# Seven transposed tiles by DMA instead of TensorE, one score step moved, and PSUM banks of pair 2 dealt anew, in a fused attention and phase-mixing kernel

## The chip, the cores and the metric

The kernel runs on one core of a Trainium2 chip. The metric is the device time of one execution in microseconds (us); of several runs the median is taken. The core's engines are TensorE (PE, matrix products), VectorE (DVE), ScalarE (ACT) and GpSimd (POOL); SyncE (SP) issues DMAs. Each engine works through its own list of instructions in order, and semaphores hold an instruction back until what it needs is done.

## The reference

Eight batches, 576 tokens, 8 heads of 64, so a model width of 512. First comes attention within chunks of 64 tokens, then a token mixer with phases and a channel product:

```python
scores = (1/8) * q_c @ k_c^T            # within each chunk of 64 tokens, per head
attn = softmax(scores)
x = (attn @ v_c), heads side by side     # (8, 576, 512)

theta = x @ w_theta
zr, zi = x * cos(theta), x * sin(theta)
y = w_tok_r @ zr + w_tok_i @ zi          # over the 576 tokens
u = x + y
out = u + max(u @ w_ch, 0)
```

## The kernel before, in words

The eight batches are taken as four pairs, 0 to 3. The two batches of a pair hold 2 x 576 tokens, that is nine tiles of 128 tokens: tiles 0 to 3 are the first batch, 4 to 7 the second, and tile 8 holds the last 64 tokens of both. The attention half works in groups of such tiles, A, B, C, D (two tiles each) and M (tile 8). The second half works by tile. Operands are fp16 and sums fp32.

The order of the work is written out by hand. `ORDER`, at the top of the file, is a list of steps such as `V1.2D.3`: a kind of step, the pair, the group or the tile, and a PSUM bank or a buffer slot. The steps are issued as they stand there, each engine receives its share in that order, and nothing reorders them. Moving a step in the list therefore moves it on its engine and on no other. The kinds that matter here, with the lines on which the profile shows them:

- `qk`, `v`: loads of a group, issued by POOL with a cast to fp16 (L170, L165, L210).
- `T`: DVE transposes queries and keys of a group (L332). `S`: TensorE makes the scores, in small tiles of 32 x 64 of its array, 64 products for a full group (L351). `E`: ACT takes the exponentials (L380).
- `V0`, `V1`: TensorE multiplies with the values, four heads each (L397, also in smaller array tiles). `N0`, `N1`: DVE takes the reciprocals (L412) and divides (L414); that gives x.
- `X`: TensorE transposes x into PSUM (L434), and `xa` or `xv` copies it out (L459, L457); or `xd`, one DMA transpose from SBUF to SBUF, issued by SP (L451).
- `H`: theta on TensorE (L472). `G`: cosine and sine on ACT (L491). `Z`: DVE multiplies x by both (L507 to L514).
- `Y`: the token product of a tile, nine TensorE products of 128x512 (L537). `A`: DVE adds x, which makes u in the place of x (L549).
- `U`: TensorE transposes u in four blocks into PSUM (L554), and `ua` (ACT, L566) or `uv` (DVE, L564) copies it out; or `ud`, one DMA transpose issued by SP (L562).
- `W`: the channel product, four TensorE products (L577). `R`: DVE takes the maximum with 0 and adds u (L589). `st`, `sg`, `sa`: the store, issued by SP, POOL or ACT (L605, L602).

The `U` and `ud` ways to the transposed u are these:

```python
    def u_t(p, j, b):
        ps = banks(b, 1, FP16)[:, 0:DM].rearrange("p (a c) -> p a c", c=P)
        for a in range(NDB):
            nc.tensor.transpose(ps[:, a, :], st["x", p][:, j, a * P : a * P + P], id16)
...
            if engine == "d":
                nc.sync.dma_start(uT, st["x", p][:, j], transpose=True)
```

PSUM has eight banks, all dealt by the numbers in `ORDER`. A step that writes a bank waits until the step that read the bank last is done. `S`, `H` and `X` of a full group use one or two banks, from the number given on. Because the two halves of the kernel overlap, the second half of pair 1 (`Y`, `U`, `W`, `R` of tiles 10 to 18, the first digit being the pair) runs between the attention steps of pairs 2 and 3. In the list before, the tiles of pair 1 are all transposed on TensorE; those of pairs 2 and 3 (but 38) by DMA. SP's list is short: stores of pair 0 and 1, the x transposes of 2C and 2D, then the u transposes of pair 2 and so on. ACT needs another function table for `E` than for `G`, and loads it whenever the kind changes (L140).

Of the kernel before, what the change touches and what calls it, by code (L numbers as in the profile page):

```python
# [48 lines left out]
A.26 E.3B.2 v.3D sa.11 ud.23.2 ud.21.4 W.16.4 A.25 R.16.1 W.13.2 V1.3D.0 R.13.2 V1.3A.6 V0.3A.3
N1.3D ua.12.1 N0.3A st.16 sa.13 xd.3M.0 N1.3A Y.24.5 A.24 Y.27.2 A.27 W.12.0 R.12.4 V0.3D.3  # L50
V1.3B.6 V0.3B.1 N1.3B xd.3A.3 ud.20.3 N0.3B N0.3D Y.28.5 V1.3C.6 V0.3C.0 A.28 W.14.2 H.3M.3
G.3M.0 R.14.0 xd.3B.1 ud.25.5 N0.3C H.3A.4 xd.3D.2 G.3A.1 W.21.2 N1.3C R.21.3 W.23.0 Z.3A H.3B.6
G.3B.2 sg.17 Z.3M ud.24.6 W.25.1 sa.21 R.23.5 xd.3C.0 H.3D.2 ud.28.7 W.20.4 H.3C.5 ud.22.1
G.3D.1 R.25.1 Z.3B Y.30.0 G.3C.0 Z.3D ud.26.0 sg.12 Z.3C Y.31.7 R.20.2 A.30 A.31 Y.36.1 Y.35.2
W.22.3 A.35 R.22.4 Y.33.5 W.28.6 A.33 Y.34.4 sg.23 A.34 ud.35.4 R.28.3 ud.31.2 W.26.0 Y.32.7
Y.37.2 W.35.3 A.36 ud.33.5 R.26.5 W.31.5 A.32 A.37 Y.38.4 ud.34.3 ud.30.1 st.26 ud.36.7 sa.20
sg.25 sa.28 R.35.1 R.31.2 ud.32.0 A.38 ud.27.4 sg.14 W.34.6 W.36.1 U.38.2 W.30.0 W.33.7 sg.31
sa.35 ua.38.3 R.34.0 ud.37.2 R.30.3 st.30 W.27.2 sa.34 R.36.5 sg.22 R.33.6 sg.36 R.27.2 W.32.3
R.32.4 W.38.5 R.38.0 sg.32 st.33 st.27 sx.38 W.24.4 R.24.3 sa.24 W0.37.6 R0.37.1 W1.37.0 R1.37.2
sa1.37 st0.37  # L60
""".split()


# [611 lines left out]
```

## Time and profile before

| | |
|---|---|
| Median of 3 runs | 191.35 us (191.06 to 191.56) |
| The profiled execution's own time | 190.84 us |
| Its span, first to last instruction | 189.0 us |
| Granted TensorE clock over the span | 0.997 |
| TensorE busy | 181.8 us, 96% |
| DVE / ACT / POOL busy | 136.8 / 95.3 / 89.7 us |
| Transposes of u on TensorE (L554) | 76 |
| DMA transposes of u / of x, issued by SP | 17 / 7 |

Lines named Lnn are lines of the kernel before. "PE" in the profile is the matrix product, "PEld" the load of its stationary operand, which overlaps. A product's length as printed holds the time of the pipeline too: products follow each other more closely than they are long, so costs are taken from one start to the next. A bracket in a row gives the idle time before it and the instruction that ended it.

### The profile page before, as it was taken

What the parts mean: (1) busy time and instruction counts of PE and PEld (TensorE: products, weight loads), DVE (VectorE), ACT (ScalarE), POOL (GpSimd) and SP (SyncE); (2) the same over time, 40 slices, a digit from 0 to 9 for tenths busy, and PEclk for the clock granted to TensorE, in tenths of its full rate; (3) what the DMA queues carried; (4) which work ended last, traced back from release to release, by engine and by line L of the source; (5) the groups of instructions that cost most, each with busy time, mean ns of one, the idle gap of its engine ahead of it and who ended that gap; (6) DMA issues with size and microseconds to landing.
All of it is one profiled execution on the core that took longest, in us unless ns stands there. A gap on an engine that the chain in (4) does not pass through costs nothing.

```text
span 189.0 us, 6110 instructions
## 1 busy us (share of the span) xinstructions
PE 181.8 (96%) x2649; PEld 93.8 (50%) x2649; DVE 136.8 (72%) x259; ACT 95.3 (50%) x124; POOL 89.7 (47%) x129
## 2 busy tenths in 40 slices
PE   7999999999999999999999999999999999999990
PEld 2446555654566465545554555465454444444440
DVE  0527886889798999699877867963987965455480
ACT  3247995276566993586109984695304680000100
POOL 8874986698876898997386410100010020000220
PEclk9999999999999999999999999999999999999998
DMA  5999999999999999999999990921457861238975
GB/s 151 295 189 173 180 172 170 190 177 169 199 187 181 192 148 224 178 144 174 212 147 175 179 129 10 243 80 63 141 140 141 183 206 59 41 78 186 266 272 186
DMA packets 98682, 31.34 MB, mean 166 GB/s; under 512 B 90336, under 2 KB 94304, under 8 KB 98656
## 3 DMA queue, kind: packets, MB, share of 16 engines
q0 software_dynamic: 75952, 18.11, 98.2%
q1 hardware_dynamic: 20560, 9.18, 20.3%
q10 hardware_dynamic: 2144, 3.67, 6.0%
q8 instruction: 20, 0.33, 0.7%
q14 instruction: 6, 0.05, 0.1%
HBM read 33.06 MB, written 9.44 MB: 225 GB/s over the span
## 4 chain that ended last, share of the span: by engine, by line
PE 74%; DMA 9%; DVE 6%; POOL 5%; issue 3%; ACT 1%; POOLq 0%; DVEq 0%
PE psum L537 31%; PE psum L577 13%; PE psum L472 13%; DMA land<-in_k_dram 8%; PE psum L154 7%; PE psum L351 4%; POOL v L210 3%; PE psum L397 3%; DMA v<-in_v_dram 2%; PE psum L554 2%; DVE T L332 1%; PE psum L284 1%; PE psum L434 1%; DVE o L589 1%; DVE x L549 1%
## 5 line engine op out<-in xcount | busy, mean ns | idle before, releaser
L537 PEld LDWEIGHTS <-wT 128*128 128x128 f16 (+1 forms) x360 | 30.7, 100 | 34.0 <-issue 1.5
L210 POOL DMA_DIRECT2D v<-in_v_dram x56 | 41.7, 763 | 11.2 <-DMA land<-in_k_dram 7.9
L537 PE MATMUL psum<-zr,wT 128*128 128x512 f16 (+1 forms) x180 | 45.4, 381 | 0.4 <-DVE x L549 0.3
L537 PE MATMUL psum<-zi,wT 128*128 128x512 f16 (+1 forms) x180 | 43.1, 379 | 0.0
L605 POOL DMA_DIRECT2D out_dram<-o x10 | 5.5, 554 | 69.4 <-DVE o L589 49.7
L549 DVE TENSOR_TENSOR x<-psum,x 128x512 f16<-128x512 f32 x36 | 24.5, 683 | 17.0 <-PE psum L537 16.3
L577 PE MATMUL psum<-wch,uT 128*128 128x512 f16 (+1 forms) x148 | 35.2, 374 | 0.0
L472 PE MATMUL psum<-wtheta,xT 128*128 128x512 f16 x144 | 34.1, 380 | 0.2 <-ACT xT L459 0.2
L589 DVE SCALAR_TENSOR_TENSOR o<-psum,x 128x512 f32<-128x512 f32 (+1 forms) x37 | 24.4, 671 | 9.5 <-PE psum L577 5.4
L491 ACT ACTIVATE cos<-psum,pihalf 128x1024 f16<-128x1024 f32 (+1 forms) x22 | 21.2, 963 | 16.3 <-PE psum L472 16.2
L332 DVE STREAM_TRANSPOSE T<-land 64x256 f32<-64x256 f32 (+3 forms) x38 | 26.9, 723 | 1.8 <-DMA land<-in_k_dram 1.4
L380 ACT ACTIVATE eT<-psum 128x1024 f16<-128x1024 f32 (+1 forms) x22 | 18.4, 864 | 19.0 <-PE psum L351 19.0
L414 DVE TENSOR_TENSOR x<-psum,recip 128x512 f16<-128x512 f32 (+1 forms) x40 | 25.5, 638 | 1.4
L566 ACT COPY uT<-psum 128x512 f16<-128x512 f16 x15 | 8.5, 593 | 32.5 <-PE psum L554 31.5
L472 PEld LDWEIGHTS <-xT 128*128 128x128 f16 x144 | 13.4, 98 | 15.6 <-ACT xT L459 0.3
L577 PEld LDWEIGHTS <-uT 128*128 128x128 f16 x148 | 13.7, 98 | 14.6 <-issue 0.4
L140 ACT ACT_TABLE_LOAD x14 | 18.0, 1283 | 4.1 <-DVE recip L412 3.1
L491 ACT ACTIVATE sin<-psum 128x1024 f16<-128x1024 f32 (+1 forms) x22 | 19.1, 870 | 0.0
L170 POOL DMA_DIRECT2D land<-in_q_dram x15 | 13.6, 907 | 5.6 <-DVE o L589 2.3
L154 PE MATMUL psum<-zeros 128*128 128x512 f16 x51 | 14.5, 445 | 1.2 <-DVE pihalf L145 1.2
L170 POOL DMA_DIRECT2D land<-in_k_dram x15 | 13.6, 904 | 1.7 <-DMA land<-in_k_dram 1.3
L351 PEld LDWEIGHTS <-T 32*64 32x64 f16 x1152 | 10.6, 105 | 4.7 <-DVE T L332 1.9
(40 smaller groups left out, 141.9 us busy)
## 6 DMA issues: line engine op xcount, KB each, us to landing
land<-in_q_dram POOLq DMA_DIRECT2D x15, 256.0 KB, 6.8
land<-in_k_dram POOLq DMA_DIRECT2D x15, 256.0 KB, 7.3
out_dram<-o SPq DMA_DIRECT2D x11, 256.0 KB, 2.7
v<-in_v_dram POOLq DMA_DIRECT2D x40, 64.0 KB, 6.2
out_dram<-o ACTq DMA_DIRECT2D x10, 256.0 KB, 2.9
out_dram<-o POOLq DMA_DIRECT2D x10, 256.0 KB, 3.2
v<-in_v_dram POOLq DMA_DIRECT2D x16, 128.0 KB, 6.9
land<-in_moe_w_theta_dram SPq DMA_DIRECT2D x2, 512.0 KB, 7.4
```

What stands on the lines that cost most here:

```text
L154: nc.tensor.matmul(banks(b), zeros[:, 0:P], zeros)
L170: nc.gpsimd.dma_start(t[:, w].rearrange("p h s d -> p h (s d)"), ap[2 * p + bb, :, s0 : s0 + GT, :].rearrange("h (p s) d -> p h (s d)", s=2),)
L210: nc.gpsimd.dma_start(v16[rows, slot + t, :, 0:D], v[b, :, t0 : t0 + m, :].rearrange("h s d -> s h d"),)
L332: nc.vector.transpose(to.bitcast(FP32).rearrange("p (x l s) -> p x s l", l=32, s=2), src.bitcast(FP32).rearrange("p (x s d) -> p x s d", s ...
L380: nc.scalar.activation(out=to, in_=ps, func=AF.Exp, scale=scale)
L414: nc.vector.tensor_tensor(out=x.rearrange("p r (h d) -> p r h d", h=H // 2), in0=ps[:, :, :, 0:D], in1=recip[:, 0:n].broadcast_to((P, n, H ...
L472: nc.tensor.matmul(ps[:, (j - js[0]) * DM : (j - js[0] + 1) * DM], xT[:, j, a, :], wtheta16[:, a, :], start=(a == 0), stop=(a == NDB - 1),)
L491: nc.scalar.activation(out=t[:, js[0] : js[-1] + 1].rearrange("p j e -> p (j e)"), in_=ps, func=AF.Sin, bias=bias, scale=1.0,)
L537: nc.tensor.matmul(ps[half[c]] if j == MID else ps, wT[:, kt, t0 : min(t0 + P, S)], z, start=(b is not None and i == 0), stop=(i == len(kt ...
L549: nc.vector.tensor_tensor(out=x, in0=st.pop(("ps_y", p, j)), in1=x, op=ALU.add)
L577: nc.tensor.matmul(ps, uT[:, a, :], wch16[:, a, cols[f]], start=(a == 0), stop=(a == NDB - 1),)
L589: nc.vector.scalar_tensor_tensor(out=o, in0=ps, scalar=0.0, in1=st["x", p][:, j, cols[f]], op0=ALU.max, op1=ALU.add,)
```

## The change

Only `ORDER` is changed; the functions are the same, and the file is one line shorter, so that L562 becomes L561 and so on.

1. For the tiles 10, 11, 12, 13, 14, 16 and 17 of pair 1, the step `U` and its copy `ua` or `uv` are taken out, and `ud` is put in with the same slot. Five of them (10, 11, 16, 13, 14) stand in a row after `xd.2C`, which itself moves up ahead of `H.2B`; `ud.17` follows `A.17`, and `ud.12` follows `W.17`. `st.05`, a store that stood ahead of `xd.2C`, is now behind `ud.17` on SP. Tiles 15 and 18 stay on TensorE.
2. `S.3B` and `E.3B` move up from behind `S.3A` and `Y.26` to behind `Y.21`, ahead of `Z.2C`, `Y.22` and the scores 3D and 3A. `R.15` moves up to ahead of `Y.20`.
3. Around pair 2's values and x: `Y.15` writes bank 7 (was 2), `X.2A` writes bank 4 (was 2); `A.14` moves behind `A.15`; each of `N0.2B`, `N1.2B` and `N0.2A` now follows its `V` in the list; `U.18` and its copy move behind `X.2A`; `V1.3M` moves from behind `Y.18` to behind `U.18`.

The part of the list that changes, cut to it:

```diff
-V0.2M.4 N0.2M v.2C V1.2C.2 V1.2M.5 W.07.0 qk.3A.11 N1.2C N1.2M R.07.2 qk.2D.12 Y.18.6 V1.3M.7
-V0.2C.0 A.18 N0.2C S.2B.4 E.2B.1 Y.14.2 A.14 V0.2B.3 V1.2B.5 V0.2A.0 N0.2B Y.15.2 U.18.3 N1.2B
-N0.2A A.15 uv.18.2 qk.3C.0 v.2D X.2B.5 X.2M.6 xa.2B.2 xa.2M.3 X.2A.2 v.3B xa.2A.0 H.2B.0 T.3C.0
-T.2D.2 G.2B.1 qk.3B.1 W.18.3 R.18.3 H.2A.5 U.15.4 Y.17.2 U.10.3 H.2M.0 Z.2B G.2A.2 ua.15.4
-ua.10.3 N1.3M G.2M.0 S.3C.5 Z.2A A.17 S.2D.3 E.2D.2 W.15.1 U.17.7 Z.2M Y.20.2 uv.17.1 V1.2D.3
-E.3C.1 A.20 V0.3M.0 V0.2D.5 st.05 Y.23.7 xd.2C.1 N1.2D A.23 N0.2D T.3B.1 U.14.2 U.11.3 sa.18
-N0.3M xd.2D.2 W.17.4 ua.11.5 U.16.7 R.15.4 st.07 Y.21.3 A.21 R.17.5 qk.3D.3 v.3C v.3A H.2C.5
-ua.16.6 T.3A.0 W.10.7 ua.14.0 G.2C.1 T.3D.2 H.2D.0 G.2D.2 Y.22.2 Z.2C R.10.0 S.3D.3 S.3A.5 st.15
-E.3A.3 S.3B.0 E.3D.0 Z.2D Y.26.7 sg.03 U.12.5 A.22 U.13.2 sa.10 ua.13.7 W.11.6 R.11.3 Y.25.3
-A.26 E.3B.2 v.3D sa.11 ud.23.2 ud.21.4 W.16.4 A.25 R.16.1 W.13.2 V1.3D.0 R.13.2 V1.3A.6 V0.3A.3
-N1.3D ua.12.1 N0.3A st.16 sa.13 xd.3M.0 N1.3A Y.24.5 A.24 Y.27.2 A.27 W.12.0 R.12.4 V0.3D.3
+V0.2M.4 N0.2M v.2C V1.2C.2 V1.2M.5 W.07.0 qk.3A.11 N1.2C N1.2M R.07.2 qk.2D.12 Y.18.6 V0.2C.0
+A.18 N0.2C S.2B.4 E.2B.1 Y.14.2 V0.2B.3 N0.2B V1.2B.5 N1.2B V0.2A.0 N0.2A Y.15.7 A.15 A.14
+qk.3C.0 v.2D X.2B.5 X.2M.6 xa.2B.2 xa.2M.3 X.2A.4 U.18.3 uv.18.2 V1.3M.7 v.3B xa.2A.0 xd.2C.1
+ud.10.3 ud.11.5 ud.16.6 ud.13.7 ud.14.0 H.2B.0 T.3C.0 T.2D.2 G.2B.1 qk.3B.1 W.18.3 R.18.3 H.2A.5
+U.15.4 Y.17.2 H.2M.0 Z.2B G.2A.2 ua.15.4 N1.3M G.2M.0 S.3C.5 Z.2A A.17 ud.17.1 S.2D.3 E.2D.2
+W.15.1 Z.2M R.15.4 Y.20.2 V1.2D.3 E.3C.1 A.20 V0.3M.0 V0.2D.5 st.05 Y.23.7 N1.2D A.23 N0.2D
+T.3B.1 sa.18 N0.3M xd.2D.2 W.17.4 ud.12.1 st.07 Y.21.3 S.3B.0 E.3B.2 A.21 R.17.5 qk.3D.3 v.3C
+v.3A H.2C.5 T.3A.0 W.10.7 G.2C.1 T.3D.2 H.2D.0 G.2D.2 Y.22.2 Z.2C R.10.0 S.3D.3 S.3A.5 st.15
+E.3A.3 E.3D.0 Z.2D Y.26.7 sg.03 A.22 sa.10 W.11.6 R.11.3 Y.25.3 A.26 v.3D sa.11 ud.23.2 ud.21.4
+W.16.4 A.25 R.16.1 W.13.2 V1.3D.0 R.13.2 V1.3A.6 V0.3A.3 N1.3D N0.3A st.16 sa.13 xd.3M.0 N1.3A
+Y.24.5 A.24 Y.27.2 A.27 W.12.0 R.12.4 V0.3D.3 V1.3B.6 V0.3B.1 N1.3B xd.3A.3 ud.20.3 N0.3B N0.3D
```

More of the change, by code (lines that the diff above doesn't have):

```diff
@@ L51 @@
[L51 to L60, printed above, removed]
+V0.2M.4 N0.2M v.2C V1.2C.2 V1.2M.5 W.07.0 qk.3A.11 N1.2C N1.2M R.07.2 qk.2D.12 Y.18.6 V0.2C.0
+A.18 N0.2C S.2B.4 E.2B.1 Y.14.2 V0.2B.3 N0.2B V1.2B.5 N1.2B V0.2A.0 N0.2A Y.15.7 A.15 A.14
+qk.3C.0 v.2D X.2B.5 X.2M.6 xa.2B.2 xa.2M.3 X.2A.4 U.18.3 uv.18.2 V1.3M.7 v.3B xa.2A.0 xd.2C.1
@@ new lines @@
+W.16.4 A.25 R.16.1 W.13.2 V1.3D.0 R.13.2 V1.3A.6 V0.3A.3 N1.3D N0.3A st.16 sa.13 xd.3M.0 N1.3A
+Y.24.5 A.24 Y.27.2 A.27 W.12.0 R.12.4 V0.3D.3 V1.3B.6 V0.3B.1 N1.3B xd.3A.3 ud.20.3 N0.3B N0.3D
+Y.28.5 V1.3C.6 V0.3C.0 A.28 W.14.2 H.3M.3 G.3M.0 R.14.0 xd.3B.1 ud.25.5 N0.3C H.3A.4 xd.3D.2
+G.3A.1 W.21.2 N1.3C R.21.3 W.23.0 Z.3A H.3B.6 G.3B.2 sg.17 Z.3M ud.24.6 W.25.1 sa.21 R.23.5
+xd.3C.0 H.3D.2 ud.28.7 W.20.4 H.3C.5 ud.22.1 G.3D.1 R.25.1 Z.3B Y.30.0 G.3C.0 Z.3D ud.26.0 sg.12
+Z.3C Y.31.7 R.20.2 A.30 A.31 Y.36.1 Y.35.2 W.22.3 A.35 R.22.4 Y.33.5 W.28.6 A.33 Y.34.4 sg.23
@@ L61 @@
+A.34 ud.35.4 R.28.3 ud.31.2 W.26.0 Y.32.7 Y.37.2 W.35.3 A.36 ud.33.5 R.26.5 W.31.5 A.32 A.37
+Y.38.4 ud.34.3 ud.30.1 st.26 ud.36.7 sa.20 sg.25 sa.28 R.35.1 R.31.2 ud.32.0 A.38 ud.27.4 sg.14
+W.34.6 W.36.1 U.38.2 W.30.0 W.33.7 sg.31 sa.35 ua.38.3 R.34.0 ud.37.2 R.30.3 st.30 W.27.2 sa.34
+R.36.5 sg.22 R.33.6 sg.36 R.27.2 W.32.3 R.32.4 W.38.5 R.38.0 sg.32 st.33 st.27 sx.38 W.24.4
+R.24.3 sa.24 W0.37.6 R0.37.1 W1.37.0 R1.37.2 sa1.37 st0.37
 """.split()
```

## The prediction

> **What bounds the kernel now.** I read the page first (busy times, the slices of TensorE, the chain that ended last), then the busy times of four stretches of the second half.
>
> ```profile
> PE 181.8 (96%) x2649; PEld 93.8 (50%) x2649; DVE 136.8 (72%) x259; ACT 95.3 (50%) x124; POOL 89.7 (47%) x129
> ...
> PE   7999999999999999999999999999999999999990
> ...
> PE 74%; DMA 9%; DVE 6%; POOL 5%; issue 3%; ACT 1%; POOLq 0%; DVEq 0%
> ```
> ```profile
> 96.00:101.00 5.00, 4.45 (x60) 2.73 (x49) 4.90 (x11) 1.72 (x3) 4.81 (x6) 1.00 1.64 150
> 101.00:113.00 12.00, 12.00 (x225) 6.44 (x224) 8.29 (x16) 11.47 (x15) 4.29 (x7) 1.00 1.77 167
> 113.00:127.00 14.00, 14.00 (x261) 7.53 (x259) 11.81 (x20) 9.25 (x12) 0.59 (x1) 1.00 0.41 97
> 127.00:184.00 57.00, 57.00 (x415) 26.67 (x413) 36.95 (x65) 14.72 (x18) 4.35 (x8) 1.00 0.56 149
> ```
>
> The columns of the second fence are the stretch and its length, then the busy time of PE, weight loads, DVE, ACT and POOL, the granted clock, the DMA share and GB/s. TensorE is never idle from 101 to 184 us, at full clock. Work taken off it there shortens the run, unless another engine or a transfer becomes late. From 96 to 101 us it does wait (4.45 of 5.00), and DVE is full (4.90). DMA is loaded until about 113 us (share 1.77) and then nearly free (0.41).
>
> **The change, part by part.** All of it lies between 92 and 131 us. I follow one shift, in us against the trace, along TensorE's order of instructions. The rows are start, length, engine, line, operation, tiles, shape and count.
>
> ```profile
> 96.47 1.02 PE L537 MATMUL psum<-zr,wT 128*128 128x512 f16 x4 [0.27 <-DVE x L549]
> ...
> 98.41 0.39 PE L554 MATMUL psum<-id,x 128*128 128x128 f16 x4
> 98.63 1.56 PE L434 MATMUL psum<-id,x 128*128 128x128 f16 x20
> 100.34 0.39 PE L472 MATMUL psum<-wtheta,xT 128*128 128x512 f16 x1 [0.15 <-ACT xT L459]
> ...
> 107.06 1.03 PE L472 MATMUL psum<-wtheta,xT 128*128 128x512 f16 x4
> 108.02 1.24 PE L351 MATMUL psum<-T 32*64 32x64 f16 x128
> 109.19 1.04 PE L577 MATMUL psum<-wch,uT 128*128 128x512 f16 x4
> ...
> 112.33 0.69 PE L397 MATMUL psum<-v,eT 64*64 64x65 f16 x40
> ...
> 114.90 0.61 PE L554 MATMUL psum<-id,x 128*128 128x128 f16 x8
> 115.34 1.03 PE L577 MATMUL psum<-wch,uT 128*128 128x512 f16 x4
> 116.21 0.39 PE L554 MATMUL psum<-id,x 128*128 128x128 f16 x4
> ```
>
> *Seven u by DMA.* A u tile costs TensorE four transposes. Eight of them start at 114.90 and the next work at 115.34: 0.22 for four (the row's 0.61 is pipelined time, not cost). Seven tiles make 7 x 0.22 = -1.54. The six ACT copies and the one DVE copy that vanish lie beside TensorE and count nothing. One gain is lost again: without U.17, V0.2D (the last of the 40 products at 112.33) would come 0.22 earlier, but it needs the exponentials E.3C, which end at 110.72 + 1.92 = 112.64 and come no earlier for that. So +0.22.
>
> ```profile
> 110.72 1.92 ACT L380 ACTIVATE eT<-psum 128x1024 f16<-128x1024 f32 x2
> ```
>
> *Pair 2's banks.* Y.15 writes bank 2, which A.14 must read first: 0.27 idle at 96.47. It now writes bank 7, and A.14 goes behind A.15 on DVE. From 98.41 to 100.34 stand 24 transposes, 6 x 0.22 = 1.32 of 1.93; the other 0.61 is waiting, for A.15 (X.2A uses bank 2 again) and for ACT's copy of xT. X.2A now uses bank 4 and needs only N0.2A, which without A.14 ahead of it (an L549 addition, 0.68 as in A.17's row below) ends that much earlier; U.18 and V1.3M now stand between X.2B and H.2B and cover the copy. I take all 0.88 as gained. The other bound is 0.27, since DVE is full here.
>
> V1.3M leaves the group behind Y.18 and stands alone, as does S.3B at its new place: TensorE changes its tile shape twice more. The price: four products take 116.21 - 115.34 = 0.87, 0.217 each, so the pair of scores at 108.02 takes 109.19 - (107.06 + 0.87) = 1.26.
>
> ```profile
> 122.69 1.03 PE L537 MATMUL psum<-zr,wT 128*128 128x512 f16 x4
> ...
> 124.73 1.80 PE L351 MATMUL psum<-T 32*64 32x64 f16 x192
> 126.46 0.82 PE L537 MATMUL psum<-zr,wT 128*128 128x512 f16 x3
> ```
>
> Three scores take 126.46 - (122.69 + 9 x 0.217) = 1.82. A score is then 0.56 and a change of shape 1.26 - 1.12 = 0.14, say 0.15; two of them, +0.30.
>
> *S.3B ahead of Y.22.* It follows Y.21 and needs its keys (T.3B) and bank 0, which N0.3M frees. Both are on DVE, behind A.23 and N0.2D.
>
> ```profile
> 115.10 0.69 DVE L549 TENSOR_TENSOR x<-psum,x 128x512 f16<-128x512 f32 x1 [1.13 <-PE psum L537]
> ...
> 117.88 0.42 DVE L414 TENSOR_TENSOR x<-psum,recip 128x256 f16<-128x256 f32 x1
> ```
>
> A.23 (the first row) reads Y.23, whose products are through at 114.90. N0.3M (the last row) ends at 118.30, 3.4 later, with DVE full in between. TensorE has only W.17 and Y.21 there, 13 x 0.217 = 2.8. So it waits 0.6, less what of the change of shape runs under it: +0.5. Bounds: 0, if DVE runs ahead, and 1.2, if one more operation of 0.68 stands ahead. R.15 goes ahead on DVE and frees bank 1 in time. E.3B now stands before G.2C on ACT, with a table load between them; G.2C is late by that, but G.2D still begins with the end of H.2D, and Y.26 has Y.22, S.3D and S.3A in front. I count 0 there.
>
> *The DMA side.* SP gets six transposes in a row (xT of 2C, then u of 10, 11, 16, 13, 14) from about 94 to 102 us, in the loads' time, and ud.17 after them.
>
> ```profile
> xT<-x SPq DMA_TRANSPOSE x1, 8.6
> ```
> ```profile
> L562 SPq DMA_TRANSPOSE uT<-x x17: 1189/1225/1412, 120.1 to 175.6; - x17
> ...
> DMA to landing us min/median/max: 2.4/2.8/4.9
> ```
> ```profile
> 107.69 0.68 DVE L549 TENSOR_TENSOR x<-psum,x 128x512 f16<-128x512 f32 x1
> ```
>
> The first row is the one xT transpose issued amid the loads (DMA issues from 84 to 100 us): 8.6 us to landing. The second view is all uT transposes, 1.2 us of issue on SP each, none before 120 us. W.10, the first reader of the five, comes after Y.21, later than 118; they have 16 us. Only ud.17 is near its reader. Its tile is finished by A.17 (the third row), which shifts by -0.88 + 0.15 and ends at 107.6. W.17 moves to 115.34 - 0.88 + 0.15 - 0.22 (U.10) - 0.44 (U.14, U.11) = 113.95, U.17's share being lost as above. That leaves 6.3 us, and a wait there is taken off the 0.5 at S.3B. Between 4.9 and 8.6 to landing I take 6: no wait. The loads that the transposes push out are pair 3's, whose keys 3B are transposed just before N0.3M's row, after 116 us; I count 0. st.05, now behind ud.17, frees a buffer that R.10 wants after W.10. xd.2D keeps its place some 5 us ahead of H.2D: 0.
>
> Sum: -1.54 + 0.22 - 0.88 + 0.30 + 0.50 = **-1.40 us**. The profiled execution took 190.84 (span 189.0), so 189.4. The median of the runs is 191.35, 0.5 above it; the time to expect there is 189.95, written **190.0**.
>
> A rule that speaks against the change: the Trainium skill, "VectorE: DVE Perf Modes", section "The three transpose paths", gives 1309 ns for a 128x128 transpose by DMA and 390 ns on TensorE, and its rules for kernel authors prefer TensorE where PSUM will do as destination. An estimate from that page: four blocks one after another are 5.2 us a tile, six tiles 31 us, and W.17 would wait some 13 us. The median of 2.8 for four blocks does not bear that out.
>
> **The rivals.**
>
> *ud.17 lands late (slower).* In the trace the transfers nearly stop where the one xT transpose runs amid the loads:
>
> ```profile
> 99.00:100.00 1.00, 0.88 (x17) 0.76 (x14) 1.00 (x3) 0.72 (x1) 1.00 (x2) 1.00 0.46 80
> ```
>
> The share is 0.46 there against 1.77 later: the transpose seems to hold the DMA engines until all have come to it. If each of the five behind the xT costs such a meeting of 3 us, the last ends near 94.3 + 8.6 + 5 x 3 = 118 and ud.17 near 121. W.17 would wait 7 us, less the 0.5: 190.0 + 6.5 = 196.5. It decides where ud.17 lands 8.2 us after its issue (6.3 + 0.5 + 1.4): there the gain is gone. For it: 8.6 was measured. Against it: that was a tile of twice the size, in deeper loads. The same crowding could catch xd.2D: 8.6 to landing against its 5 us of room, 190.0 + 3.6 = 193.6. The Trainium skill, "DMA: Bandwidth & Descriptors", section "Queues, rings and completion order", says that an engine changes between queues only after a whole packet; the 8.6 against 2.8 agrees with such a wait.
>
> *DVE stays the limit (no change).* Its order is dealt anew, its work hardly. If X.2A and H.2B still wait for it, 0.27 of the 0.88 is gained, 190.6; with S.3B's wait at its bound of 1.2, 191.3. For it: 4.90 of 5.00 busy. Against it: A.14 and V1.3M no longer stand ahead of X.2A.
>
> *Everything gains.* No wait at S.3B and U.17's share kept: 190.0 - 0.72 = 189.3.
>
> **How the numbers follow.** A measurement here can tell about 0.3%, 0.57 us, from no change. The forecast with the better case (189.3 to 190.7): 0.58. DVE stays the limit: 0.14. Late transposes: 0.28, of which 0.03 end within 0.3% and 0.03 still faster. Faster is 0.55 from the first, 0.02 from the second and 0.03: 0.60. Within 0.3% is 0.03 + 0.12 + 0.03 = 0.18, slower 0.22. The range reaches down to 189.0 (the better case, less the 0.3 by which a run lies below the median) and up to 193.0, where xd.2D's case nearly fits and ud.17's middle does; about 0.15 is left out.
>
> **What would show it.** Right: the u transposes (L554) fall from 76 to 48; no wait by DVE before Y.15, none by ACT before H.2B; one wait of about 0.5 before S.3B; TensorE busy otherwise to its end. Wrong: idle TensorE ahead of W.17 or H.2D, ended by a DMA of uT or xT; uT landings over 8 us around 108; or DVE still named ahead of X.2A.

## The result, and the profile after

The changed kernel takes 193.03 us (median of 4 runs, 192.95 to 193.80), the kernel before 191.33 on the same chip. The ratio is 1.0111, with a 95% interval of 1.0088 to 1.0134. So it is slower, by 1.7 us between the medians and by 1.1% in the ratio, where 190.0 had been forecast. The profiled execution is the longest of the four: 193.80 us, span 191.7. Ratios here and below leave out executions more than 1.5% above the fastest of their kernel (among them five of e3's ten, two of e1's ten and the profiled ones of e2 and e11); where a transfer lands now early, now late, this takes out late ones too, so medians and spreads, which hold all, stand beside them.

The page of the changed kernel, in the same parts as before, with the group of the channel product (its last column is idle time ahead of it and what ended that):

```profile
PE 181.3 (95%) x2621; PEld 92.3 (48%) x2621; DVE 136.8 (71%) x258; ACT 92.0 (48%) x118; POOL 89.6 (47%) x129
...
PE   7898999999999999999999986999999999999990
...
PEclk9999999999999999999999996999999999999999
...
PE 68%; DMA 20%; DVE 6%; issue 2%; POOL 1%; ACT 0%; SPq 0%; DVEq 0%; POOLq 0%
...
L576 PE MATMUL psum<-wch,uT 128*128 128x512 f16 (+1 forms) x148 | 36.1, 380 | 2.5 <-DMA uT<-x 2.5
```

TensorE has 28 products fewer (seven tiles of four transposes), and its row of nines now has an 8 and a 6 past the middle, with the clock row down to 6 in the same place (the two 8s near the start lie ahead of the change). The share of DMA in the chain that ended last has doubled, from 9% to 20%. The same four stretches as in the prediction, in the same columns:

```profile
96.00:101.00 5.00, 5.00 (x71) 3.10 (x59) 4.84 (x10) 2.28 (x3) 4.64 (x7) 1.00 1.68 146
101.00:113.00 12.00, 11.85 (x218) 6.07 (x216) 9.83 (x18) 10.42 (x14) 3.97 (x6) 1.00 1.75 149
113.00:127.00 14.00, 11.54 (x106) 4.90 (x105) 7.64 (x12) 4.70 (x6) 1.58 (x3) 0.88 1.26 200
127.00:184.00 57.00, 57.00 (x528) 26.68 (x526) 37.67 (x66) 16.32 (x19) 3.79 (x7) 1.00 0.58 135
```

The first stretch has lost its waits (5.00 busy, against 4.45), as forecast. The third is where it went wrong: 11.54 busy of 14, at a clock of 0.88, with a DMA share of 1.26 where it had been 0.41. TensorE's instructions in order of time, cut to those that matter:

```profile
96.12 1.04 PE L536 MATMUL psum<-zr,wT 128*128 128x512 f16 x4
97.00 1.24 PE L536 MATMUL psum<-zi,wT 128*128 128x512 f16 x5
98.07 1.28 PE L433 MATMUL psum<-id,x 128*128 128x128 f16 x20
...
99.79 1.90 PE L471 MATMUL psum<-wtheta,xT 128*128 128x512 f16 x8
...
113.90 0.38 PE L536 MATMUL psum<-zr,wT 128*128 128x512 f16 x1
116.74 1.89 PE L576 MATMUL psum<-wch,uT 128*128 128x512 f16 x4 [2.46 <-DMA uT<-x]
118.42 1.86 PE L536 MATMUL psum<-zr,wT 128*128 128x512 f16 x4
120.12 1.03 PE L536 MATMUL psum<-zi,wT 128*128 128x512 f16 x4
120.98 0.38 PE L536 MATMUL psum<-zr,wT 128*128 128x512 f16 x1
121.29 0.81 PE L350 MATMUL psum<-T 32*64 32x64 f16 x64
122.04 1.90 PE L471 MATMUL psum<-wtheta,xT 128*128 128x512 f16 x8
```

TensorE stands idle for 2.46 us ahead of W.17 (116.74) until u.17 lands, that is, until the semaphore tells that the transfer is done. From start to start, 113.90 to 116.74 is 2.84 where a product takes 0.22, so 2.62 are lost. Then its four products, and the next four, follow one another at 0.42 (118.42 - 116.74 = 1.68 for four) instead of 0.216: half rate, 0.82 + 0.83 = 1.65 us more for the eight. The chain of waits through this place names the transfer, and two single DMA issues (around 108 and 116 us) give the landings, in us from issue:

```profile
107.34 0.50 ACT cos L490
107.84 8.85 DMA uT<-x
116.69 0.05 issue
116.74 1.89 PE psum L576 x4
```
```profile
uT<-x SPq DMA_TRANSPOSE x1, 8.9
```
```profile
xT<-x SPq DMA_TRANSPOSE x1, 5.5
```

ud.17 took 8.9 us, not the 6 that I had taken. The transpose xd.2D took 5.5, against 3.4 before; it wasn't waited for here only because TensorE was already late by more. What the six transposes in a row did to the loads is seen in the DMA issues from 92 to 110 us, of the kernel before and then of the changed one (median us to landing):

```profile
v<-in_v_dram POOLq DMA_DIRECT2D x3, 128.0 KB, 9.0
v<-in_v_dram POOLq DMA_DIRECT2D x6, 64.0 KB, 7.3
...
xT<-x SPq DMA_TRANSPOSE x1, 8.6
```
```profile
v<-in_v_dram POOLq DMA_DIRECT2D x5, 64.0 KB, 13.2
v<-in_v_dram POOLq DMA_DIRECT2D x2, 128.0 KB, 14.9
...
uT<-x SPq DMA_TRANSPOSE x6, 8.7
xT<-x SPq DMA_TRANSPOSE x1, 7.5
```

The loads of values take some 6 us longer; the last of them, v.3D, landed at 120.4 us where it had landed at 112.7. So both u.17 and xT of 2D are under way in a time that is still full of loads, where before the loads were done by 113.

The whole difference, from the start of Y.14 to the start of the last product, is 92.60 against 89.93, +2.67 us. By starts of the same products in both traces:

| on to the start of | difference, us | what makes it |
|---|---|---|
| H.2B (from Y.14) | -0.54 | banks |
| H.2M | -0.23 | U.10 is gone |
| Y.20 | -0.22 | U.17 is gone |
| Y.23 | +0.23 | V0.2D waits for E.3C |
| Y.21 | +2.76 | the wait 2.62, half rate 0.82, less three u |
| H.2C | +1.68 | half rate 0.83, S.3B is now here |
| H.2D and Y.22 | +0.01 | |
| Y.26 | -0.56 | S.3B is gone from here |
| Y.25 | -0.45 | U.12 and U.13 are gone |
| the end | 0.00 | |

This is the longest of the four executions, set against an execution of the kernel before that lies 0.5 below its median. A stretch of 3.4 us at half rate lowers the granted clock over the span by 0.009, and of the four only this one (0.991) has room for it: the others, 0.7 to 0.9 us shorter, are on record with 0.993, 0.994 and 1.000. So the 1.65 us belong to this execution. What makes up the others' loss no trace shows; e15 against e14, below, prices the early reader by their medians.

### The profile page after: what moved, and what is told of

It reads as the page before. It is cut to its first block, busy times and chain, and to the rows that moved or that the text cites. A ratio compares the mean times of both kernels' runs of the same rounds, so it can differ in the third digit from the quotient of the medians.

```text
span 191.7 us, 6050 instructions
## 1 busy us (share of the span) xinstructions
PE 181.3 (95%) x2621; PEld 92.3 (48%) x2621; DVE 136.8 (71%) x258; ACT 92.0 (48%) x118; POOL 89.6 (47%) x129
## 4 chain that ended last, share of the span: by engine, by line
PE 68%; DMA 20%; DVE 6%; issue 2%; POOL 1%; ACT 0%; SPq 0%; DVEq 0%; POOLq 0%
PE psum L536 30%; PE psum L471 15%; PE psum L576 12%; DMA land<-in_k_dram 8%; DMA uT<-x 5%; PE psum L350 3%; DMA land<-in_q_dram 3%; PE psum L396 3%; PE psum L433 2%; DMA v<-in_v_dram 2%; DMA out_dram<-o 2%; DVE o L588 2%; DVE T L331 2%; PE psum L283 2%; PE psum L553 1%
## 5 line engine op out<-in xcount | busy, mean ns | idle before, releaser
L536 PE MATMUL psum<-zr,wT 128*128 128x512 f16 (+1 forms) x180 | 46.2, 386 | 0.1
L576 PE MATMUL psum<-wch,uT 128*128 128x512 f16 (+1 forms) x148 | 36.1, 380 | 2.5 <-DMA uT<-x 2.5
L565 ACT COPY uT<-psum 128x512 f16<-128x512 f16 x9 | 5.2, 592 | 27.8 <-PE psum L553 27.8
L153 PE MATMUL psum<-zeros 128*128 128x512 f16 x51 | 13.1, 412 | 1.2 <-DVE pihalf L144 1.2
```

Source lines behind the costliest of these rows:

```text
L536: nc.tensor.matmul(ps[half[c]] if j == MID else ps, wT[:, kt, t0 : min(t0 + P, S)], z, start=(b is not None and i == 0), stop=(i == len(kt ...
L576: nc.tensor.matmul(ps, uT[:, a, :], wch16[:, a, cols[f]], start=(a == 0), stop=(a == NDB - 1),)
```

## The experiments

In the traces below "landed" is read from single DMA issues. The theory after the result was: the transposes amid the loads are slow themselves and push the loads some 7 us back; u.17's reader comes too early for that; and the idle time costs the clock too. The rival: something else in the change (the banks, S.3B's place, the loads that come late) costs the time.

### e1: u.17 on TensorE again

```diff
-Z.2A A.17 ud.17.1 S.2D.3 E.2D.2 W.15.1 Z.2M R.15.4 Y.20.2 V1.2D.3
+Z.2A A.17 S.2D.3 E.2D.2 W.15.1 U.17.7 Z.2M R.15.4 Y.20.2 uv.17.1 V1.2D.3
```

> Only u of tile 17 goes back to TensorE (U.17.7 behind W.15, its copy on DVE behind Y.20); the other six stay DMA transposes. Theory 'one late tile': all of the loss is the wait of W.17 for the DMA transpose of u 17 (2.6 us idle) and the half clock after it (8 products of 0.43 instead of 0.22, 1.7 us). Then W.17 starts right behind Y.23, about 0.5 us of waiting appear before S.3B, and the time is 193.0 - 4.3 + 0.5 = 189.2, at most 189.6. Rival 'crowding': the six transposes in the loads' time hold up more than this one reader (xT of 2D, pair 3's keys and values), so the time stays above 191.

Measured: 192.03 us (190.23 to 196.46, 10 runs) against 190.88 for the kernel before, ratio 1.0024 (0.9991 to 1.0056): the rival's time. W.17's wait is gone, and so is a good part of the loss, but nothing is gained. TensorE in order of time shows two new waits:

```profile
117.55 0.70 PE L349 MATMUL psum<-T 32*64 32x64 f16 x64 [0.49 <-DVE x L412]
...
123.47 1.90 PE L470 MATMUL psum<-wtheta,xT 128*128 128x512 f16 x8 [2.52 <-DMA xT<-x]
```

The first is S.3B's wait for N0.3M, 0.5 as forecast (it had been hidden under W.17's). The second is H.2D's for xT of 2D, which was issued at 115.97 and landed 7.5 us later. My expectation had kept the zero for this transfer: it is the second step of the prediction that fell.

### e2: TensorE kept busy ahead of W.17

```diff
-N0.3M xd.2D.2 W.17.4 ud.12.1
+N0.3M xd.2D.2 dm.13.4 W.17.4 ud.12.1
```

> The changed kernel with 13 products on zeros (the step dm, bank 4) ahead of W.17, 13 x 0.217 = 2.8 us, so that TensorE isn't idle while it waits for u 17. Theory 'the idle time costs the clock': W.17 starts when u 17 lands as before, but at full clock, so 1.7 us come back: 191.4. Rival 'the clock fell for another reason' (or it fell already in the profile only): still 193.0. If the late landing were caused by TensorE itself, the start of W.17 would move as well.

Measured: 193.63 us (192.39 to 196.24, 6 runs), ratio 1.0103 (1.0068 to 1.0138): not the 191.4 of my theory. The products behind W.17 are at full rate, but in the profiled execution H.2D waited 2.27 us for xT of 2D, and the half rate came there. So e2 didn't price the clock; e16 tries again.

### e3: W.10 and W.17 change places

```diff
-xd.2D.2 W.17.4 ud.12.1 st.07 Y.21.3 S.3B.0 E.3B.2 A.21 R.17.5 qk.3D.3 v.3C
-v.3A H.2C.5 T.3A.0 W.10.7 G.2C.1 T.3D.2 H.2D.0 G.2D.2 Y.22.2 Z.2C R.10.0
+xd.2D.2 W.10.4 st.07 Y.21.3 S.3B.0 E.3B.2 A.21 R.10.0 qk.3D.3 v.3C
+v.3A H.2C.5 T.3A.0 W.17.7 ud.12.1 G.2C.1 T.3D.2 H.2D.0 G.2D.2 Y.22.2 Z.2C R.17.5
```

> W.10 and W.17 change places on TensorE (and R.10, R.17 on DVE, ud.12 behind W.17); all seven u stay DMA transposes. u 10 landed at 104.5 in the changed kernel, u 17 at 116.7; W.10's place is now at about 114, W.17's about 119. Theory 'one late tile': nobody waits for a u, 0.5 us of waiting before S.3B, 189.2 to 189.6, and the transpose of u 17 still lands 8 to 9 us after its issue. Rival 'crowding': above 191, with a wait at another DMA's reader (H.2D for xT of 2D, landed 121.5).

Measured: 193.0 us (189.79 to 196.32, 10 runs), the rival's time; the ratio, 0.9999 (0.9963 to 1.0034), is that of the five shorter executions alone. In the profiled execution (191.12) no u is waited for, although u.17 landed 9.0 us after its issue; H.2D waits 0.51 for xT of 2D. The times spread over 6.5 us: the kernel before has 1.4. That suggests a transfer that lands at different times and stands close to its reader.

### e4: the five others behind ud.17

```diff
-xa.2A.0 xd.2C.1 ud.10.3 ud.11.5 ud.16.6 ud.13.7 ud.14.0 H.2B.0
+xa.2A.0 xd.2C.1 H.2B.0
...
-A.17 ud.17.1 S.2D.3
+A.17 ud.17.1 ud.10.3 ud.11.5 ud.16.6 ud.13.7 ud.14.0 S.2D.3
```

> The five transposes of u 10, 11, 16, 13, 14 are issued behind that of u 17 instead of ahead of it. Theory 'queue': u 17 was late because it stood behind five others; alone behind xT of 2C it lands within 6 us of its issue (by 114), W.17 doesn't wait, and the time is 189.2 to 190, if u 10 lands before its reader at about 118.5. Rival 'loads': any transpose issued amid the loads takes 8 to 9 us, as xT of 2C did in both kernels (8.6 and 7.6); u 17 still lands at about 116.5, W.17 waits 2.5 us, 193 or, with u 10 late as well, more.

Measured: 191.36 us (190.73 to 191.85, 10 runs), ratio 1.0019 (1.0000 to 1.0039), between the two times that I gave. With none of the five ahead of it u.17 lands in 6.7 us, and W.17 waits 0.26; but xd.2D now stands behind five others on SP's queue and H.2D waits for it:

```profile
114.22 1.04 PE L574 MATMUL psum<-wch,uT 128*128 128x512 f16 x4 [0.26 <-DMA uT<-x]
...
122.09 1.25 PE L469 MATMUL psum<-wtheta,xT 128*128 128x512 f16 x5 [1.42 <-DMA xT<-x]
```

### e5: the banks alone

```diff
-Y.14.2 A.14 V0.2B.3 V1.2B.5 V0.2A.0 N0.2B Y.15.2 U.18.3 N1.2B N0.2A A.15 uv.18.2
+Y.14.2 V0.2B.3 N0.2B V1.2B.5 N1.2B V0.2A.0 N0.2A Y.15.7 A.15 A.14
...
-xa.2M.3 X.2A.2 v.3B
+xa.2M.3 X.2A.4 U.18.3 uv.18.2 V1.3M.7 v.3B
```

> The kernel before with part 3 of the change alone: pair 2's banks, the order of its N steps and A.14, U.18, V1.3M. All u of pair 1 by TensorE, S.3B in its old place. The forecast's terms: 0.88 us of waiting gone, 0.15 for one more change of the tile shape, so 0.7 us less than before, 190.2 if before is 190.9. The trace of the changed kernel shows Y.15 without idle time and about 0.05 ahead of H.2B. Rival 'DVE stays the limit': only 0.27 comes through, less 0.15: within 0.2 us of before.

Measured: 190.49 us (189.92 to 191.23, 12 runs) against 190.97, ratio 0.9982 (0.9969 to 0.9996). Faster, by 0.3 us in the ratio and 0.5 between the medians, less than the 0.7 expected. From the start of Y.14 to the last product the trace has 89.37 instead of 89.93, -0.56. The part that only dealt banks and turns anew is a gain by itself.

### e6: S.3B alone

```diff
-W.17.4 ua.11.5 U.16.7 R.15.4 st.07 Y.21.3 A.21
+W.17.4 ua.11.5 U.16.7 st.07 Y.21.3 S.3B.0 E.3B.2 A.21
...
-E.3A.3 S.3B.0 E.3D.0
+E.3A.3 E.3D.0
...
-A.26 E.3B.2 v.3D
+A.26 v.3D
```

R.15 moves up with it, as in the change.

> The kernel before with part 2 alone: S.3B and E.3B behind Y.21, R.15 ahead of Y.20. Here U.14, U.11 and U.16 still stand between Y.23 and Y.21, 0.66 us more TensorE work, so N0.3M is in time and S.3B waits at most 0.1. Forecast: 0.15 for the change of shape, so 0.1 to 0.3 us more than before. If the earlier scores were worth something by themselves (E.3B out of the later ACT work), it would be below before.

Measured: 191.94 us (191.53 to 192.94, 6 runs), ratio 1.0058 (1.0036 to 1.0080). Slower, by more than expected. Of some 1.0 us, 0.2 is the change of shape (Y.21 to H.2C is 0.74 longer, Y.22 to Y.26 0.55 shorter), some 0.3 isn't seen in the trace, and 0.5, from start to start, is a wait of U.12:

```profile
129.62 0.61 PE L552 MATMUL psum<-id,x 128*128 128x128 f16 x8 [0.35 <-ACT eT L378]
```

U.12 writes the bank that E.3A reads, and E.3A comes later on ACT because E.3B now runs ahead of G.2C with a table load between (1.28 us at 121.81). In the changed kernel U.12 is gone, so this wait is not part of its loss.

### e7: five of the transposes after the loads

The banks as in e5; u of 11, 16, 13, 12 and 14 by DMA, issued behind xd.2D at some 117 us; u of 10 and 17 on TensorE; S.3B in its old place; R.15 as in the change. The main line of the edit:

```diff
-N0.2D T.3B.1 U.14.2 U.11.3 sa.18 N0.3M xd.2D.2 W.17.4 ua.11.5 U.16.7 R.15.4 st.07
+N0.2D T.3B.1 sa.18 N0.3M xd.2D.2 ud.11.5 ud.16.6 ud.13.7 W.17.4 ud.12.1 ud.14.0 st.07
```

> Part 3 whole, part 2 undone, and five of the seven u (11, 16, 13, 12, 14) by DMA, but issued behind xT of 2D at about 117 us, when the loads are through; u of 10 and 17 on TensorE. Theory 'crowding by transposes amid the loads': nothing is issued amid the loads that wasn't before, so xT of 2D lands about 3.5 us after its issue, no reader of a u waits (first one at about 127), and the gains add up: 0.7 from the banks, 5 x 0.22 = 1.1 from TensorE: 1.8 us less than before, 189.1 if before is 190.9. Rival 'DMA transposes cost by themselves' (they hold up stores or later transposes wherever they stand): less than 0.7 us below before.

Measured: 190.33 us (189.75 to 191.77, 12 runs) against 190.97, ratio 0.9970 (0.9950 to 0.9991). Faster than both kernels, but by about a third of what was expected, inside the rival's bound of 0.7. From Y.14 to H.2C the trace is 1.22 us shorter than before; then H.2D waits:

```profile
118.86 1.03 PE L575 MATMUL psum<-wch,uT 128*128 128x512 f16 x4
120.70 1.47 PE L470 MATMUL psum<-wtheta,xT 128*128 128x512 f16 x6 [0.82 <-DMA xT<-x]
```

With the queue free of u and the loads done, xT of 2D still takes 4.5 us, and TensorE is now early enough to feel it. V0.2D waits for E.3C, N0.2D follows it, and xd.2D is issued only then (116.2 here, 116.8 before): time taken off TensorE ahead of H.2D doesn't bring xT forward by as much.

### e8: five transposes that nobody reads

```diff
-xa.2A.0 H.2B.0
+xa.2A.0 xd.2C.1 ud.10.3 ud.11.5 ud.16.6 ud.13.7 ud.14.0 H.2B.0
...
-Y.23.7 xd.2C.1 N1.2D
+Y.23.7 N1.2D
```

Everything else is as before, U steps included; the five write buffers that are not read.

> The kernel before with the five transposes of u 10, 11, 16, 13, 14 issued in addition, behind xT of 2C amid the loads, into the buffers that are written again from TensorE later: their result isn't read, and the products keep their order. Theory 'crowding': the loads of pair 3 end some 5 to 8 us later than the 112.7 of before, xT of 2D is issued as before at about 117 but amid them, lands at 122 to 125 instead of 120.2, H.2D waits 1 to 4 us, and the time is 1 to 5 us above before, with a wide scatter. Rival 'only a late reader costs': as before, within 0.3 us.

Measured: 191.87 us (190.25 to 193.12, 8 runs), ratio 1.0037 (1.0009 to 1.0064), between the two expectations. The loads go back by as much as in the changed kernel (issues from 92 to 110 us):

```profile
v<-in_v_dram POOLq DMA_DIRECT2D x5, 64.0 KB, 13.7
v<-in_v_dram POOLq DMA_DIRECT2D x2, 128.0 KB, 15.0
...
uT<-x SPq DMA_TRANSPOSE x5, 8.6
```

v.3D landed at 119.9 instead of 112.7: 7.2 us later with five transposes of 128x512. That is the most it can be: in the kernels that put no u transpose among the loads (before, e5, e6, e7, e9) v.3D landed at 112.7 to 116.5, the latest in e6, whose loads already ran some 3 us later than before at 87 us. So five transposes cost the last load 3.4 to 7.2 us. It is the transposes amid the loads that move the loads, not anything else in the change. In the profiled execution (191.11) xT of 2D landed 0.5 us ahead of H.2D and nothing waited; what made other executions longer isn't seen.

### e9: e7 with Y.22 ahead of H.2D

```diff
-T.3D.2 H.2D.0 G.2D.2 Y.22.2 Z.2C
+T.3D.2 Y.22.2 H.2D.0 G.2D.2 Z.2C
...
-S.3B.0 E.3D.0 Z.2D Y.26.7
+E.3D.0 Z.2D Y.26.7 S.3B.0
```

> The kernel of e7 (five transposes behind the loads, banks dealt anew, no move of S.3B) with Y.22 put ahead of H.2D, and S.3B's place behind Y.26 as in the kernel before. In e7 H.2D waited 0.97 us for xT of 2D (issued 116.21, landed 120.7). My theory: this transfer has become what ends last, so 1.94 us of other products (Y.22: nine of them at 216 ns) ahead of H.2D cover the wait, and the gain made ahead of H.2C (1.22 us in e7) passes: 1.2 to 1.8 us faster than the kernel before, 189.2 to 189.8, with no wait of H.2D for xT of 2D. Rival: the chain behind H.2D (its exponentials and Z.2D) is as tight; then the same 0.6 us as in e7 is gained, 190.3, and a wait shows at Z.2D or Y.26.

The second part of the edit moves S.3B behind Y.26 (in the kernel before it stood ahead of it), one more change of shape than in e7.

Measured: 190.46 us (189.93 to 191.28, 12 runs), ratio 0.998 (0.9967 to 0.9993). The rival held: xT of 2D is no longer waited for, and the time is that of e7, within the intervals. The chain behind H.2D is the next one; W.11 waits for E.3A, which ACT reaches after G.2D:

```profile
128.16 1.02 PE L575 MATMUL psum<-wch,uT 128*128 128x512 f16 x4 [0.25 <-ACT eT L378]
```

From start to start the waits at Y.26 and W.11 lose 0.26 and 0.32. How much of W.11's comes from S.3B's move isn't told apart.

### e10 and e11: the transposes amid the loads, with Y.22 ahead of H.2D

e10 is e1 with S.3B behind Y.26 and E.3B behind A.26, as in e9; e11 is e3. Both have this edit:

```diff
-T.3D.2 H.2D.0 G.2D.2 Y.22.2 Z.2C
+T.3D.2 Y.22.2 H.2D.0 G.2D.2 Z.2C
```

> The kernel of e1 (six transposes amid the loads, u.17 on TensorE, banks dealt anew) with S.3B back in its old place and Y.22 ahead of H.2D. My theory: transposes amid the loads cost only through readers that come too early for them; with u.17 on TensorE and H.2D 1.94 us later none is left, so 1.5 to 2.0 us faster than the kernel before, 189.0 to 189.5, and little scatter. Rival: the late loads cost elsewhere too, or xT of 2D takes up to 9.5 us as in e2 and is late still: 190.5 or more, with a wait at H.2D or at the first readers of pair 3's loads.

> The kernel of e3 (all seven transposes, W.10 and W.17 changed round, S.3B early) with Y.22 ahead of H.2D. My theory: e3 lost 0.67 us at H.2D to xT of 2D in its profiled execution, and its times were spread over several us because that transfer lands at different times from one execution to the next; with 1.94 us more room 189.0 to 190.0, and less spread than e3. Rival: the spread comes from u.17's landing (9.0 us after its issue in e3, with W.17 only just behind it) or from the loads; then the spread stays, and the median stays at 191 or above.

Measured: e10 190.7 us (189.82 to 193.07, 12 runs) against 190.89, ratio 0.9993 (0.9972 to 1.0014); e11 192.98 us (191.52 to 195.68, 6 runs), ratio 1.0091 (1.0055 to 1.0128). Both missed the time that my theory gave; their rivals gave it. In e10's profiled execution xT of 2D landed after 4.2 us and nothing waited for it; in e11's it landed after 9.2, with v.3D's last part landing 0.8 earlier, and H.2D waited 2.27 in spite of its later place. 1.94 us of room are not enough for a landing that moves by 5.

### e12: u.17 alone by DMA

```diff
-Z.2A A.17 S.2D.3 E.2D.2 W.15.1 U.17.7 Z.2M Y.20.2 uv.17.1 V1.2D.3
+Z.2A A.17 ud.17.1 S.2D.3 E.2D.2 W.15.1 Z.2M Y.20.2 V1.2D.3
```

The rest is e5, with xd.2C where the change has it.

> The kernel before with the banks dealt anew (as in e5) and u.17 alone by DMA, the other six on TensorE. It tells apart what made u.17 land 8.9 us after its issue: if it was the queue of transposes and the loads they had pushed back, it lands within 6 us here, W.17 doesn't wait, and the time is that of e5 less 0.2 us, about 190.2. If the loads alone do it, it lands 8 to 9 us after its issue again, W.17 waits 2 us or more, and the time is 191.5 or above.

Measured: 190.67 us (190.53 to 191.77, 10 runs) against 190.89, ratio 0.9999 (0.9986 to 1.0013), 0.5 above what I expected. The single DMA issue and W.17 (the row of 114.73):

```profile
uT<-x SPq DMA_TRANSPOSE x1, 5.9
```
```profile
114.28 0.61 PE L552 MATMUL psum<-id,x 128*128 128x128 f16 x8
114.73 1.03 PE L575 MATMUL psum<-wch,uT 128*128 128x512 f16 x4
```

5.9 us and no wait: with the five others not ahead of it, u.17 lands when I had said. The 8.9 belongs to the five and to the loads that they push back; e4, with none of them ahead, agrees with its 6.7. From Y.14 to the last product it has 89.38 against e5's 89.37, so U.17 gives nothing of its own, because V0.2D waits for E.3C, as the prediction's +0.22 said.

### e13 and e14: xT of 2D by TensorE

e13 is e7, e14 is e3 (all seven u by DMA amid the loads, W.10 ahead of W.17), both with X.2D and a copy by ACT in the place of xd.2D:

```diff
-N0.3M xd.2D.2
+N0.3M
...
+X.2D.7 xa.2D.2
```

In e13 the new steps stand ahead of H.2C, in e14 ahead of S.3B.

> The kernel of e7 with xT of 2D made by TensorE (eight 128x128 transposes ahead of H.2C and a copy by ScalarE) instead of the DMA transpose that H.2D waited for. My theory: up to H.2C e7 gained 1.22 us and lost most of it to that one landing; eight transposes cost 0.45 to 0.6 us, and no H.2D wait is left, so 0.5 to 0.8 us faster than the kernel before, 190.1 to 190.5, with less spread than e7 (189.75 to 191.77). Rival: ScalarE and VectorE behind H.2D are the limit as in e9, or the copy is late: 190.5 to 191, with a wait of 0.3 us or more at H.2D, Y.26 or W.11.

> The kernel of e3 (all seven transposes amid the loads, W.10 ahead of W.17, S.3B early) with xT of 2D made by TensorE as in e13. My theory: the transposes amid the loads cost only through two late readers, W.17 and H.2D; here the first reads later and the second doesn't read a transpose, so the loads' delay is paid by nobody: 0.8 to 1.4 us faster than the kernel before, 189.5 to 190.2, and a spread under 1.5 us where e3 had 6.5. Rival: the delayed loads of pair 3 or u.17's landing cost time by themselves; then the spread stays at 3 us or more, the median at 191 or above, and the profile shows TensorE waiting for a load or for u.17.

Measured: e13 190.16 us (189.63 to 192.29, 12 runs) and e14 190.47 us (189.93 to 191.10, 12 runs) against 191.02; ratios 0.9967 (0.9936 to 0.9997) and 0.9967 (0.9944 to 0.9990). Both are faster than both kernels. In e13 the transposes no longer stood behind xd.2D on SP and three of them were issued at 96 to 100 us, amid the loads again, so it isn't the case without crowding that I had meant. Its profiled execution, 189.63, has no wait and 88.71 from Y.14 to the last product, 1.22 less than before, but its times spread no less than e7's. e14 decides the open question. TensorE in order of time:

```profile
114.41 1.03 PE L575 MATMUL psum<-wch,uT 128*128 128x512 f16 x4
...
117.21 0.61 PE L432 MATMUL psum<-id,x 128*128 128x128 f16 x8
117.87 0.70 PE L349 MATMUL psum<-T 32*64 32x64 f16 x64
118.51 1.90 PE L470 MATMUL psum<-wtheta,xT 128*128 128x512 f16 x8
120.24 1.03 PE L575 MATMUL psum<-wch,uT 128*128 128x512 f16 x4
121.11 1.89 PE L470 MATMUL psum<-wtheta,xT 128*128 128x512 f16 x8
```

u.17 lands 8.9 us after its issue, v.3D at 121.4, no earlier than in the changed kernel, and nothing waits for a transfer: the spread is 1.2 us where e3 had 6.5. So the crowding costs TensorE time through readers that come too early, W.17 and H.2D, and pair 3's late loads cost none in this trace (e8's 0.4% without a wait in its trace stays open). The gain, 0.55 us by the medians and 0.81 in the trace from Y.14 to the last product, falls short of what I expected: X.2D takes 0.45 of it, S.3B waits 0.1 (0.66 from X.2D to S.3B, 0.54 in e15), and the scores behind Y.22 take 0.34 longer (1.52 against 1.18 in e15).

### e15 and e16: the price of the early reader, and of the clock

e15 is the changed kernel with X.2D on TensorE, so that only W.17 reads too early; e16 adds the thirteen products ahead of it.

```diff
-N0.3M xd.2D.2 W.17.4 ud.12.1 st.07 Y.21.3 S.3B.0
+N0.3M W.17.4 ud.12.1 st.07 Y.21.3 X.2D.7 xa.2D.2 S.3B.0
```
```diff
-N0.3M W.17.4 ud.12.1
+N0.3M dm.13.4 W.17.4 ud.12.1
```

> The changed kernel with xT of 2D made by TensorE as in e14, and nothing else: u.17 is read by W.17 ahead of Y.21 again. Set against e14 it prices that one reader. My theory: W.17 waits 2 to 2.6 us and the products behind it run at half rate for another 0.8 to 1.7 us, so 2.5 to 4 us slower than e14, 193.0 to 194.5. Rival: most of the loss was H.2D's late xT in executions other than the profiled one; then 191 to 191.5 here.

> As e15, with thirteen products of zeros (2.8 us, no part of the computation) ahead of W.17, so that TensorE isn't idle while u.17 is on its way. Set against e15 it prices the clock alone, with the late reader at H.2D gone that spoiled e2. My theory: the half rate is lost to idle time, so it vanishes: 0.8 to 1.7 us faster than e15, 191.8 to 193. Rival: the half rate comes from something else (the data's landing, the executions' state); then no faster than e15.

Measured: e15 193.5 us (191.91 to 197.27, 6 runs), ratio 1.0112 (1.0079 to 1.0146); e16 192.78 us (192.21 to 193.15, 6 runs), ratio 1.0086 (1.0066 to 1.0107), both against 190.90. e15 against e14, which differ in the places of W.10 and W.17, is 1.0112 - 0.9967 = 1.45%, 2.8 us, in the range that I gave. Its profiled execution is the fastest of its six, and in it the products behind the wait keep full rate (four starts in 0.87):

```profile
116.25 1.04 PE L575 MATMUL psum<-wch,uT 128*128 128x512 f16 x4 [2.22 <-DMA uT<-x]
117.12 1.03 PE L535 MATMUL psum<-zr,wT 128*128 128x512 f16 x4
```

Five of the six lie in two groups, 191.91 and 192.06, and 193.36 to 193.83, some 1.6 apart, which looks like the 1.65 of eight products at half rate. The recorded clocks bear that out only in part: 193.64 and 193.83 (0.990 and 0.991) have room for such a stretch, but 193.36 is on record with 1.000. So the half rate can't be the whole of that distance. In e16 the two groups are gone (192.21 to 193.15), no execution's clock is below 0.992, and W.17 follows the products of zeros at full rate:

```profile
114.33 2.97 PE L152 MATMUL psum<-zeros 128*128 128x512 f16 x13
117.14 1.03 PE L575 MATMUL psum<-wch,uT 128*128 128x512 f16 x4
118.00 1.03 PE L535 MATMUL psum<-zr,wT 128*128 128x512 f16 x4
```

They take 2.81 where e15 waited 2.38 from start to start, so 0.43 was added, and the median is still 0.7 lower. The intervals of the two ratios overlap, though, so that difference, the price of the clock, isn't shown.

## Why the prediction was wrong, point by point

- **ud.17's landing: wrong, and it decides.** "Between 4.9 and 8.6 to landing I take 6: no wait." It was 8.9 (changed), 9.0 (e3), 8.9 (e14), 6.7 with the others behind it (e4), 5.9 alone (e12). The room that I worked out, 6.3 us, was right: W.17's place came at 114.1, A.17's end at 107.8. The mistake was to price one transpose without the five that the same change puts ahead of it, and the loads that those push back. That the lone one took 5.9 is luck: 6 was picked between two bounds. The rival "ud.17 lands late" had the mechanism, and its turning point, 8.2 us, was passed; its 3 us for each meeting was too much (the five cost the last load 0.7 to 1.4 each), so its 196.5 was too high.
- **The price of the wait: left out.** I counted a late landing as so many microseconds of idle TensorE. In the profiled execution 2.62 of idle cost another 1.65 at half rate. So the loss needn't grow evenly with the landing: near a wait of 2.4 us it can jump by that. In the other three executions the recorded clocks leave no room for it, so it explains the trace and not the median.
- **xd.2D "keeps its place some 5 us ahead of H.2D: 0": wrong.** Those 5 us are right (4.8 in e1), but its landing took 3.6 (e8) to 9.6 us (e2) where transposes had pushed the loads, and 4.5 (e7) even where the u transposes stood behind it. In the changed kernel this is hidden under W.17's wait; with that gone it takes the gain (e1, e4, e7).
- **"The loads that the transposes push out ... I count 0": right for the readers of the loads** (e14: nothing waits for them), wrong for what shares their time: the loads still on their way at 108 to 120 us stand beside u.17 and xT of 2D.
- **Pair 2's banks, -0.88 + 0.15 for V1.3M: right in kind, 0.2 too much.** -0.54 in the changed trace, -0.56 alone (e5). No wait for DVE or ACT shows there any more; from 98.07 to 99.79, 24 transposes and V1.3M take 1.72.
- **Seven u at 0.22: right.** U.10, U.17, U.12 and U.13 show as 0.22 or 0.23 each in the starts. **U.17's share lost to E.3C, +0.22: right:** e12, without U.17, is 0.01 from e5.
- **S.3B, +0.5 for the wait and 0.15 for the shape: right in size, but out of sight.** The wait was 0.49 in e1 and e3; in the changed kernel W.17's stall covered it. The shape cost 0.2.
- **DVE stays the limit: refuted** by the first stretch, where TensorE no longer waits though DVE is busy 4.84 of 5.00. **Everything gains: no.**

In the profiled execution the forecast of -1.40 and the +2.67 of the trace are 4.07 apart. W.17's wait and the half rate add 4.27 and the banks 0.2, the wait at S.3B, which didn't come, takes 0.5 off, and 0.1 is left. Had every landing been as in e12 (5.9 and 3.5 us), neither W.17 nor H.2D, 4.8 us behind its transfer's issue in e1, would have waited; no run shows that case. The versions that gain most end at 0.9967 to 0.9970, some 0.6 us: e7, e13 and e14, one not told from another by these runs. e14 is the changed kernel but for W.10 ahead of W.17 and xT of 2D on TensorE.

## What to carry to other kernels

A transfer's time to landing belongs to the moment as much as to the transfer (5.9 to 9.3 us for u.17 here): when a change adds several transfers to a busy stretch, price the last of them, and every other transfer with a reader close behind, with the new ones in front. Look for the next latency that is hidden only by the work being removed: here H.2D's operand, a chain through VectorE and a DMA, capped the gain as soon as TensorE was faster. And if the parts of a change can be separated, cost and run them so: here the part with the least to it (the banks) was a gain by itself, and a late reader elsewhere hid it.

## What was unexpected in the hardware

DMA transposes amid casting loads push those loads back: with five transposes of 128x512 the last load landed at 119.9 us (e8), without them at 112.7 to 116.5. How a transpose holds the loads up isn't shown by these runs. The transposes' own landings, and their neighbour's:

| kernel | u.17, issue to landing | xT of 2D, issue to landing | v.3D landed | xT of 2D landed |
|---|---|---|---|---|
| before | - | 3.4 | 112.7 | 120.2 |
| e12, u.17 alone | 5.9 | 3.5 | 116.1 (last landing on record; one part's is missing) | 119.6 |
| changed | 8.9 | 5.5 | 120.4 | 121.5 |
| e3 | 9.0 | 5.4 | 121.0 | 122.1 |
| e2 | 9.1 | 9.6 | 124.9 | 125.0 |
| e10 | - | 4.2 | 119.7 | 120.7 |
| e11 | 9.3 | 9.2 | 124.6 | 125.4 |
| e1 | - | 7.5 | 125.5 | 123.4 |

In four of these kernels (changed, e3, e10, e11) xT of 2D lands 0.8 to 1.1 us behind the last values of 3D, in e2 0.1; in e1, where v.3D was issued behind it, it lands ahead of them. That is an order seen, not a cause tested.

The half rate after a wait is not a matter of its length alone. Counted from start to start beyond the usual spacing, 2.62 us (changed) brought it, 2.44 (e11) and 2.43 (e2) too; 2.38 (e15) and 2.68 (e1) did not. What sorts these five is where the wait lies. In the clock records of all five traces each stretch at full clock lasts a whole number of times 3.413 us (19 to 54 times), and the half clock amid the work lasts 3.413 us, once. So the clock seems to change only at the ends of windows of that length. Counted on from the first record of each trace, in us:

| kernel | wait | window around it, or end of a window in it | half rate |
|---|---|---|---|
| changed | 114.12 to 116.74 | 113.28 to 116.69 | yes |
| e11 | 123.05 to 125.49 | 122.19 to 125.60 | yes |
| e2 | 122.66 to 125.09 | 122.42 to 125.83 | yes |
| e15 | 113.87 to 116.25 | a window ends at 114.94 | no |
| e1 | 120.79 to 123.47 | a window ends at 121.55 | no |

The three waits that lie in one window (the first but for 0.05 us) were followed by the half rate; the two that reach over the end of a window were not. That is what five traces show; no run moved a wait to test it.

The Trainium skill, "TensorE: Matmul & The Clock Gate", Part 1, speaks of an idle window of about 3.4 us that runs freely, so that the point of change varies from run to run. The windows of 3.413 us in these traces agree with that. But the gaps here were all shorter than 3.4 us, and shorter than the 3 us or so beyond which its section "Why this matters for your kernels" warns of gaps. By these runs a gap of 2.4 us isn't safe.
